# DeltaNet and a gated FFN on one core: K of two more chunks turned by VectorE, and the whole order planned anew

## The chip, the cores and the metric

The kernel runs on one core of a Trainium2 chip. The core's engines used here are TensorE (PE: matmuls, with its weight loads PEld), VectorE (DVE), ScalarE (ACT), GpSimd (POOL) and SyncE (SP, which here issues most DMAs). Each has an instruction queue of its own that it works through in order; semaphores make one wait for another. The time is the device time of one execution in microseconds. A lower time is better.

## The reference

```
def _attn_ref(q, k, v, beta):                 # (4, 8, 768, 48) each, beta (4, 8, 768)
    k_n = k / (np.linalg.norm(k, axis=-1, keepdims=True) + 1e-06)
    state = zeros((B, H, D, D))
    for t in range(S):
        kt, vt, bt = k_n[:, :, t], v[:, :, t], beta[:, :, t, None]
        y[:, :, t] = einsum('bhd,bhde->bhe', q[:, :, t], state)
        v_old = einsum('bhde,bhd->bhe', state, kt)
        state = state + bt[:, :, :, None] * einsum('bhd,bhe->bhde', kt, vt - v_old)
...
def _moe_ref(x, w_gate, w_val, w_out, rms_g): # x is y as (3072, 384)
    xn = x / sqrt(mean(x * x) + 1e-06) * rms_g
    g = xn @ w_gate                            # (384, 1536)
    return (g * sigmoid(g) * (xn @ w_val)) @ w_out
```

There are 32 heads of 48 numbers and 768 steps in time. All is fp32, except that the three weight matrices arrive as float64.

## The kernel before

**Tiling.** Time is cut into 12 chunks of 64 steps, numbered 0 to 11 here and in the code, so that the seventh and eighth chunk are 6 and 7. Within a chunk the recurrence is done as matrix products: the keys are normed (`norms`), K and Q are turned so that the head's numbers lie on the partitions (`kt`, `qt`), scores K·K and K·Q are formed on TensorE (`score_products`, L704), the triangular system of the chunk is solved on VectorE in 15 double steps (`invert`: multiply at L1070, reduce at L1076, after a scaling at L1023), the solution goes through DRAM into block form (`dx`, `dxt` to `mt`, `x2bd`, `m1bd`), and `recur` does the products with the state (L1199), the solve's application (L1281, evacuated at L1351), the output (L1317) and the state's update (L1404, added at L1522). The chunk's 256 output rows are then normed, turned and sent through the FFN. Chunks 0 and 1 use plain FFN matmuls (`ffn_plain`, L1558 and L1540). From chunk 2 on, `ffn` does the three by three block product with 15 products per half (L1651), whose results VectorE adds (L1661) and ACT copies (L1663), and `down` does a Strassen-like product with the output weights (L1708).

**How K is turned.** `kturn(c)` scales K on GpSimd (L969) and then takes one of two ways, by the constant `KSQ`. For `c < KSQ`, `turn` has TensorE transpose eight 128x128 blocks into two PSUM banks (L685), which ACT copies to `kt` (L697). For later chunks K is written to DRAM (`dsq`), read back in four DMAs with its 32x32 squares put at their turned places in the tile `q2`, and VectorE transposes every square in one instruction (`square_turn`, L715). Q of chunk 2 and later has always gone that way: 16 DMAs bring it from DRAM into the same tile `q2`, and the same L715 turns it into `qt`. So K's squares must wait until Q's have been turned, and the other way round.

**The first stretch.** The first chunks, the conversion of 18 pieces of float64 weights to fp32 by VectorE (L607, L610, L615, L639, with an ACT step at L619) and the FFN of chunks 0 and 1 share the time before the steady state. In the first 70 planned microseconds TensorE is fed idle matmuls on the identity in every planned gap (`filler`, L1826).

**What sets the order.** No order is written out by hand. Every operation is recorded in a `Plan` with its engine, a cost in microseconds, what it reads and writes, its PSUM banks and a priority or due time. `Plan.run` makes a list schedule (`forward`), goes back through it to set new priorities (`backward`), and repeats this `ROUNDS[0]` times with random shifts. Then each number in `MOVES` is the seed of one random change of the priorities (`shake`), after which the schedule is made again. The best schedule found by the planner's own costs is emitted, and each engine's queue holds its instructions in that order. So the costs in `P.add` move no work themselves, but they decide which instruction stands before which. A DMA has an issue cost (`dur`) on its queue and a cost on the shared DMA engines (`work`).

Of the kernel before, what the change touches and what calls it, by code (L numbers as in the profile page):

```python
# [22 lines left out]
STRETCH = {"PE": 1.5, "ACT": 1.5, "DVE": 1.4, "POOL": 1.2, "SP": 1.0}  # L23
ENGINES = ("PE", "ACT", "DVE", "POOL", "SP")
OVERLAP = {"PE": 0.0, "ACT": 0.1, "DVE": 0.08, "POOL": 0.06, "SP": 0.0}
ROUNDS, MOVES = (8, 3), (8000067, 8000597, 8000948, 8001017, 8002724, 8006360, 8008220, 8019300, 8029128, 8041120, 8046040, 8061420, 8103060, 8171660, 8171980, 8172520, 8176051, 8186548, 8187777, 8188940, 8197021, 8197169, 8200311, 8221546, 8225628, 8270861, 8283640, 8284428, 8285760, 8285870, 8288410, 8295221, 8301729, 8305291, 8310247, 8324080, 8458740, 8499977, 8522895, 8527737, 8540674, 8542770, 8573880, 8576584, 8577340, 8579620, 8580620, 8594840, 8603040, 8637560, 8655411, 8656870, 8664720, 8672920, 8873930, 8885129, 8893086, 8956398, 8960108, 9314698, 9382016, 9442358, 9601943)
BLOCK, ASKED, LACKED = 256, 140, 193
REACT, TURN, LAND = 2.4, 3.45, 2.6
STICK = 1.0
JKQ, JQM, JTM, JMK = 3, 99, 5, 99  # L30
EARLYN = (3, 4)
RELEASE = (4.7, 10.0, 13.0, 16.0, 16.0, 30.0, 33.0)
KSQ, XSQ = 8, 4
DRAIN, REFILL, GRACE = 0.1, 0.2, 0.0
SHAKE = 0.12
SPARE = 0.5
# [308 lines left out]
def kernel(  # L345
# [17 lines left out]
    nc = tc.nc  # L363
# [21 lines left out]
    half = sbt("half", [128, 16])  # L385
# [23 lines left out]
    q2t = q2.rearrange("p x e -> p (x e)").rearrange("p (u g th e) -> p u g th e", u=8, g=2, th=2)  # L409
    q2k = [("q2", i) for i in range(16)]  # L410
# [19 lines left out]
    AK = [("acc", 0), ("acc", 1)]  # L430
# [17 lines left out]
    ms = sbt("ms", [128, 2, 2], 2)  # L448
    rs = sbt("rs", [128, 2], 2)
# [29 lines left out]
    P = Plan()  # L479
    V = lambda n: 0.13 + 0.0011 * n  # L480
    VF = lambda n: 0.13 + 0.0006 * n
    A = lambda n: 0.2 + 0.0008 * n
    G = lambda n: 0.15 + 0.0022 * n

    def dma(dst, src, prio, r=(), w=(), work=0.3, dur=0.5, eng="SP", after=0.0):
        queue = nc.scalar if eng == "ACT" else nc.sync
        op = P.add(eng, dur, lambda: queue.dma_start(out=dst, in_=src), prio, r, w, lat=0.7)  # L487
        op.dma, op.work, op.ready, op.port = True, work, after, False
        return op

# [2 lines left out]
    def due(c, lead):  # L493

        return (64.0 - min(lead, 64.0)) if c == 0 else (90.0 if c == 1 else 152.9 + PERIOD * (c - 2)) - lead
# [156 lines left out]
    def load(c, what):  # L652
        t0 = c * C
        pk, pq, pv = ((-5, 1, 12), (5, 29, 36))[c] if c < 2 else (due(c, 150), due(c, 99), due(c, 70))
        if "q" in what and c > 1:
            for d, eh, g, th in itertools.product(range(2), repeat=4):
                e0, e1 = 32 * eh, min(D, 32 * eh + 32)
                src = q.rearrange("b (yh a) t e -> a t (b yh) e", a=4)[2 * d + g, t0 + 32 * th : t0 + 32 * th + 32, :, e0:e1]
                r0 = 64 * d + 32 * eh
                dma(q2t[r0 : r0 + 32, :, g, th, 0 : e1 - e0], src, pq, w=[q2k[8 * d + 4 * eh + 2 * g + th]], work=0.33 if eh else 0.43, after=due(c, 85))  # L660
        for key, t, src, pr in (("k2", k2[c % NK], k, pk), ("q2", q2, q, pq)):
            for g in range(2):
                if key[0] not in what or key == "q2" and c > 1:
                    continue
                dst = t[64 * g : 64 * g + 64, :, 0:D]
                s = src.rearrange("b (y g) t e -> g t (b y) e", g=2)[g, t0 : t0 + C]
                op = dma(dst, s, pr, w=[(key, c % NK, g)] if key == "k2" else q2k[8 * g : 8 * g + 8], dur=0.7, work=1.18, eng="ACT" if c == 0 and (g or key == "q2") else "SP", after=((0.0, 1.4, 0.0), (5.0, 40, 0.0))[c]["kqv".index(key[0])] if c < 2 else 44.5)
                op.lat += LATE if c == 1 or key == "q2" else 1.2 if c == 0 else 0.0
        if "v" in what and c < 2:
            for g in range(2):  # L670
                s = v.rearrange("b (y g) t e -> g t (b y) e", g=2)[g, t0 : t0 + C]
                dma(vt[64 * g : 64 * g + 64], s, pv, w=[("v", g)], dur=0.7, work=1.18, after=30 if c else 8).lat += LATE
        elif "v" in what:
            for bb in range(2):
                s = v[2 * bb : 2 * bb + 2, :, t0 : t0 + C, :].rearrange("p h t e -> t (p h) e")
                dma(vt[64 * bb : 64 * bb + 64], s, pv, w=[("v", bb)], dur=0.85, work=1.18, after=due(c, 75))
# [106 lines left out]
    def prep16(c):  # L783
        pr = 8.0 if c == 1 else 0.0
        pd = pr + (1 if c else 0)
        pi = (1.0, 45.0)[c]
        i2, ikq = c, c
# [10 lines left out]
        psf = Group()  # L798
# [57 lines left out]
        ab = [("ab", c, n) for n in range(4)]  # L856
        ak = [("acc", c)]
# [15 lines left out]
                nc.scalar.copy(flat(side)[:, L * c : L * c + 33 * 15 + 1 : 33], share())  # L873

        P.add("ACT", 0.6, start, pd, r=["half"], w=ak)
        P.add("ACT", 0.4, start2, pd + 0.5, r=[psf], w=ak, last=psf)
        x, xkeys = x16[c], [("xs", c)]
        diag = a16[c].rearrange("p j t -> p (j t)")[:, 1 : 1 + 34 * 7 + 1 : 34]
        pair = x.rearrange("p i t -> p (i t)")[:, 0:128].rearrange("p (j k) -> p j k", k=L // 2)
# [17 lines left out]
        for j in range(0, L - 2, 2):  # L897
            n, m = j + 2, L - 2 - j

            def step(j=j, n=n, m=m):  # L900
                old, new, lo = (3, 0, 1) if j % 4 else (0, 3, 0)
                cols = slice(L * c + j + 2, L * c + L)
                nc.vector.tensor_tensor(
                    out=acc[:, 1:3, 0:n, cols].rearrange("p a i t -> p i a t"),
                    in0=sides[old][:, 0:n, j : j + 2, None].to_broadcast([128, n, 2, m]),
                    in1=a16[c][:, None, j : j + 2, j + 2 : L].to_broadcast([128, n, 2, m]),
                    op=ALU.mult,
                )
                nc.vector.tensor_reduce(
                    out=acc[:, new, 0:n, cols],  # L910
                    in_=acc[:, lo : lo + 3, 0:n, cols].rearrange("p a i t -> p i t a"),
                    axis=AXL.X,
                    op=ALU.add,
                )

            P.add("DVE", 0.47 + 0.0052 * n * m, step, pi, r=ab, w=ak)

        xflat = x.rearrange("p i t -> p (i t)")

# [5 lines left out]
                else:  # L925
                    nc.vector.tensor_copy(out=dst, in_=src)

        P.add("ACT" if c else "DVE", 0.97 if c else 0.55, spread, pi, r=ak, w=xkeys)
        P.add("DVE", V(256), lambda: nc.vector.transpose(out=turned[1], in_=xflat), pi, r=xkeys, w=["turn1"])
        psb = Group()  # L930

# [12 lines left out]
        for h in range(2):  # L944
            dst = dg[c][:, 8 * h : 8 * h + 8].rearrange("p x (n m) -> p x n m", n=4)
            src = lambda h=h: psb.t[:, 128 * h : 128 * h + 128].rearrange("p (x m) -> p x m", x=8)[:, :, None].to_broadcast([128, 8, 4, L])
            w = [("dg", c, h)] + (kkall if c else [])
# [62 lines left out]
    def invert(c):  # L1010
        pd = due(c, 110) + 1
        pi = due(c, 80)
        i2, ikk = c % 2, c % 2
        dk = dkk[c % 2]
        dkeys = [("dkk", c % 2, g, i) for g in range(2) for i in range(2)]
        for par in range(2):
            dma(at_[64 * par : 64 * par + 64].rearrange("p j t -> p (j t)"),
                dk.rearrange("i g x j t -> (i g x) (j t)"), pd, r=dkeys, w=[("at", par)] + [(n_, p_, z) for n_ in ("ab",) for p_ in range(2) for z in range(4)] + [("xs", 0), ("xs", 1)], dur=0.56, work=0.95)
        bt = beta_b[:, c]
        bkeys = [("beta", i) for i in range(8)]  # L1020

# [14 lines left out]
                        bt[rows, par : W : 2],  # L1036
                    )

        P.add("ACT", 1.0, start, pd, r=["half"], w=AK)
        P.add("ACT", 0.9, start2, pd + 0.5, r=bkeys, w=AK)  # L1040


# [22 lines left out]
        for j in range(0, W - 2, 2):  # L1065
            n, m = j // 2 + 1, W - 2 - j

            def step(j=j, n=n, m=m):
                old, new, lo = (3, 0, 1) if j % 4 else (0, 3, 0)
                nc.vector.tensor_tensor(  # L1070
                    out=acc[:, 1:3, 0:n, j + 2 : W].rearrange("p a i t -> p i a t"),
                    in0=acc[:, old, 0:n, j : j + 2, None].to_broadcast([128, n, 2, m]),
                    in1=at_[:, None, j : j + 2, j + 2 : W].to_broadcast([128, n, 2, m]),
                    op=ALU.mult,
                )
                nc.vector.tensor_reduce(  # L1076
                    out=acc[:, new, 0:n, j + 2 : W],
                    in_=acc[:, lo : lo + 3, 0:n, j + 2 : W].rearrange("p a i t -> p i t a"),
                    axis=AXL.X,
                    op=ALU.add,  # L1080
                )

            P.add("DVE", 0.47 + 0.0052 * n * m, step, pi, r=[("at", 0), ("at", 1)], w=AK)

        def spread(dst, op, turn):
            for side in range(2):
# [90 lines left out]
    def recur(c):  # L1177
# [245 lines left out]
        for h in halves:  # L1423
            gy = groups(psy, h)

            if c == 0:
                p = h[0]
                for g in range(2):
                    P.add("ACT", A(192) + 0.15, lambda p=p, g=g: nc.scalar.activation(
                        out=xflat[:, 128 : 320], in_=psy[g, p].t[:, 192 * p : 192 * p + 192], func=ACTF.Square,  # L1430
                        scale=1.0 / math.sqrt(DM), accum_out=ms[i2][:, p, g : g + 1],
                    ), py, r=[psy[g, p]], w=[("x1", 1), ("ms", i2, p)], last=psy[g, p])
# [21 lines left out]
                    nc.gpsimd.tensor_scalar(out=ms[i2][:, cols, 0], in0=ms[i2][:, cols, 0], scalar1=ms[i2][:, h[0], 1:2], scalar2=1e-6, op0=ALU.add, op1=ALU.add)  # L1454
                nc.gpsimd.tensor_tensor(out=rs[i2][:, cols], in0=ms[i2][:, cols, 0], in1=mhalf[:, cols], op=ALU.pow)

            P.add("POOL", 1.1, root, py, r=["half"], w=[(k_, i2, p) for p in h for k_ in ("ms", "rs")])
            if c == 0:
                p = h[0]
                P.add("DVE", V(128), lambda p=p: nc.vector.tensor_scalar(  # L1460
# [401 lines left out]
```

## Time and profile before

| | |
|---|---|
| time, median of 3 runs | 673.76 us (672.74 to 675.8) |
| profiled execution, its own time | 673.21 us |
| its span, first to last instruction | 671.5 us |
| TensorE busy | 657.3 us, 98% of the span, granted clock 0.994 |
| VectorE busy | 577.0 us, 86% |
| ACT busy | 298.2 us, 44% |
| POOL busy | 88.5 us, 13% |
| K and Q transposes on TensorE, L685 | 64 and 16 matmuls |
| square transposes on VectorE, L715 | 10 for Q at 1.238 us, 4 for K at 1.241 us |

An engine's busy time is the time in which it has an instruction under way; for TensorE the ends are modelled, since its matmuls overlap. The profiled execution's time is 1.7 us longer than its span, for what lies before the first and after the last instruction. A wait is shown with the instruction that waited, what released it, its total, how often and the longest. The chain of waits follows the last instruction back to what released it, and so on; each piece has its start, its length and its line. In a table of windows each row has the stretch, its length, the busy time and instructions of PE, PEld, DVE, ACT and POOL, the granted TensorE clock, the DMA engines' share and GB/s.

### The profile page before, as it was taken

Reading aid. Unit: us, or ns where it says so; the run is one execution under the profiler, and the core shown is the slowest. Engines: PE = TensorE matmul, PEld = TensorE weight load, DVE = VectorE, ACT = ScalarE, POOL = GpSimd, SP = SyncE. Lnnn points to the kernel's source line nnn. Section 1 sums busy time; section 2 is a strip of 40 time slices with the busy share of each in tenths; the row PEclk is TensorE's granted clock in tenths of the full one; section 3 lists DMA queues with packets and bytes.
Section 4 is the critical chain, followed back from the end, with each engine's and each line's share of the span. In section 5 each row is a group of like instructions: output and inputs, shape, how many; then the busy total and the mean of one; then the engine's idle time right before and its main releaser. Section 6 shows DMA issues by size and latency. Waiting matters only on the chain.

```text
span 671.5 us, 23512 instructions
## 1 busy us (share of the span) xinstructions
PE 657.3 (98%) x10070; PEld 608.2 (91%) x10070; DVE 577.0 (86%) x1199; ACT 298.2 (44%) x685; POOL 88.5 (13%) x105
## 2 busy tenths in 40 slices
PE   9899989999999999999999999999999999999997
PEld 6788768787799999999999999999999999999997
DVE  6999889999999998997998898899998798457472
ACT  7554343454235455355345345345345354343241
POOL 4212211050300040040031030030040010000000
PEclk9999979999999999999999999999999999999999
DMA  9483666573325336345347456476346434102100
GB/s 233 125 221 108 135 166 167 91 146 75 48 63 79 63 84 107 57 99 91 54 123 109 76 132 96 82 168 97 48 117 92 84 79 70 26 2 48 24 1 24
DMA packets 261822, 62.31 MB, mean 93 GB/s; under 512 B 248627, under 2 KB 253782, under 8 KB 261718
## 3 DMA queue, kind: packets, MB, share of 16 engines
q1 hardware_dynamic: 258438, 60.02, 45.5%
q8 instruction: 79, 1.29, 0.8%
q10 hardware_dynamic: 3280, 0.79, 0.6%
q14 instruction: 25, 0.20, 0.1%
HBM read 44.25 MB, written 16.52 MB: 91 GB/s over the span
## 4 chain that ended last, share of the span: by engine, by line
PE 79%; DVE 12%; SPq 3%; DMA 2%; issue 2%; ACT 1%; POOL 1%; DVEq 0%; POOLq 0%
PE bank L1651 36%; PE bank L1708 19%; PE bank L1558 7%; PE bank L1540 4%; PE bank L704 3%; PE bank L1199 3%; SPq L487 3%; PE bank L1281 1%; PE bank L1317 1%; DVE tmp L1661 1%; DVE acc L1076 1%; PE bank L685 1%; PE bank L1404 1%; PE bank L1124 1%; DVE acc L1070 1%
## 5 line engine op out<-in xcount | busy, mean ns | idle before, releaser
L1651 PE MATMUL bank<-xf,w_in 128*128 128x128 f32 x1440 | 177.4, 276 | 0.0
L1651 PEld LDWEIGHTS bank<-xf,w_in 128*128 128x128 f32 x1440 | 168.7, 192 | 0.8
L1661 DVE TENSOR_TENSOR tmp<-tmp,bank 128x512 f32<-128x512 f32 x180 | 121.3, 683 | 34.6 <-PE bank L1651 30.2
L1651 PE MATMUL bank<-xf,more 128*128 128x128 f32 x960 | 123.8, 277 | 0.0
L1651 PEld LDWEIGHTS bank<-xf,more 128*128 128x128 f32 x960 | 115.1, 192 | 0.9
L1663 ACT COPY tmp<-bank 128x512 f32<-128x512 f32 x120 | 69.0, 584 | 63.0 <-PE bank L1651 49.4
L1667 ACT ACTIVATE tmp<-tmp 128x256 f32<-128x256 f32 x120 | 50.1, 417 | 93.7 <-DVE tmp L1661 93.2
L1076 DVE TENSOR_REDUCE acc<-acc 128x30 f32<-128x90 f32 (+4 forms) x150 | 70.9, 472 | 5.2
L731 POOL TENSOR_TENSOR knrm<-ksum,half 128x16 f32<-128x16 f32 x12 | 35.5, 2960 | 274.5 <-DVE ksum L730 274.5
L1708 PE MATMUL bank<-wo_sb,hf 128*128 128x192 f32 x360 | 63.8, 329 | 0.0
L1708 PEld LDWEIGHTS bank<-wo_sb,hf 128*128 128x128 f32 x360 | 58.1, 190 | 0.5
L1070 DVE TENSOR_TENSOR acc<-acc,at 128x60 f32<-128x60 f32 (+4 forms) x150 | 52.7, 351 | 2.4
L1668 DVE TENSOR_TENSOR hf<-tmp 128x256 f32<-128x256 f32 x120 | 49.0, 418 | 5.5 <-ACT tmp L1667 4.7
L1540 PE MATMUL bank<-wo_sb,hf 128*128 128x384 f32 x96 | 35.2, 506 | 0.0
L1558 PE MATMUL bank<-xf,w_in 128*128 128x256 f32 x144 | 34.6, 387 | 0.0
L1558 PE MATMUL bank<-xp,w_in 128*128 128x256 f32 x144 | 33.4, 383 | 0.0
L1558 PEld LDWEIGHTS bank<-xp,w_in 128*128 128x128 f32 x144 | 26.8, 190 | 4.6 <-DVE more L1616 0.2
L1558 PEld LDWEIGHTS bank<-xf,w_in 128*128 128x128 f32 x144 | 26.4, 190 | 4.4 <-issue 0.2
L1713 ACT COPY tmp<-bank 128x192 f32<-128x192 f32 x30 | 9.5, 316 | 41.7 <-PE bank L1708 41.2
L1540 PEld LDWEIGHTS bank<-wo_sb,hf 128*128 128x128 f32 x96 | 18.3, 196 | 9.9 <-issue 0.6
L1096 POOL COPY acc<-acc 128x128 f32<-128x128 f32 x40 | 18.8, 500 | 63.1 <-DVE acc L1076 62.8
L1510 DVE TENSOR_TENSOR xf<-xf 128x256 f32<-128x256 f32 (+1 forms) x70 | 24.7, 381 | 2.5 <-ACT xf L1475 1.9
(198 smaller groups left out, 985.8 us busy)
## 6 DMA issues: line engine op xcount, KB each, us to landing
at<-dkk SPq DMA_DIRECT2D x20, 256.0 KB, 3.7
more<-in_moe_w_gate_dram SPq DMA_DIRECT2D x6, 768.0 KB, 7.6
vt<-in_v_dram SPq DMA_DIRECT2D x24, 192.0 KB, 4.0
k<-in_k_dram SPq DMA_DIRECT2D x23, 192.0 KB, 4.2
out_dram<-tmp SPq DMA_DIRECT2D x46, 96.0 KB, 2.2
more<-in_moe_w_val_dram SPq DMA_DIRECT2D x5, 768.0 KB, 8.4
more<-in_moe_w_out_dram SPq DMA_DIRECT2D x5, 768.0 KB, 5.5
dyn<-yn SPq DMA_DIRECT2D x16, 192.0 KB, 2.0
```

The source lines that it names most:

```text
L731: P.add("POOL", 2.95, lambda: nc.gpsimd.tensor_tensor(out=knrm[i2], in0=ksum[i2], in1=half, op=ALU.pow), pn, r=[("ksum", i2), "half"], w=[ ...
L1070: nc.vector.tensor_tensor(out=acc[:, 1:3, 0:n, j + 2 : W].rearrange("p a i t -> p i a t"), in0=acc[:, old, 0:n, j : j + 2, None].to_broadc ...
L1076: nc.vector.tensor_reduce(out=acc[:, new, 0:n, j + 2 : W], in_=acc[:, lo : lo + 3, 0:n, j + 2 : W].rearrange("p a i t -> p i t a"), axis=A ...
L1510: P.add("DVE", V(128 * n), lambda dst=dst, a=a, b_=b_, op=op: nc.vector.tensor_tensor(out=dst, in0=a, in1=b_, op=op), pxv, r=[("xp", 0)], ...
L1540: nc.tensor.matmul(po[p].t[:, 0:DM], hf[:, spot(f), 128 * p : 128 * p + 128], wo_sb[:, spot(f)], start=(f == f0), stop=(f == f1 - 1), skip ...
L1558: nc.tensor.matmul(ps.t[:, TOK * side : TOK * side + TOK], w_in[:, side, h_, 3 * t + i_, n : n + 128], x_[:, 2 * t : 2 * t + 2].rearrange( ...
L1651: nc.tensor.matmul(g.t[:, 128 * z : 128 * z + 128], fac[:, side, 128 * f : 128 * f + 128], xf[:, xs], start=(begin and z == 0), stop=False ...
L1661: P.add("DVE", V(512), lambda t=t, g=g: nc.vector.tensor_tensor(out=t, in0=t, in1=g.t, op=ALU.add), -1, r=[g], w=[tk], last=g)
L1663: P.add("ACT", A(512), lambda t=t, g=g: nc.scalar.copy(t, g.t), -1, r=[g], w=[tk], last=g)
L1667: P.add("ACT", A(256), lambda t=t: nc.scalar.activation(out=t[:, 0:256], in_=t[:, 0:256], func=ACTF.Silu), -1, w=[tk])
L1668: P.add("DVE", V(256), lambda t=t, f0=f0, p=p: nc.vector.tensor_tensor(out=hf[:, spot(f0) : spot(f0) + 2, 128 * p : 128 * p + 128], in0=t[ ...
L1708: nc.tensor.matmul(g.t[:, 0:192], a_[:, f], b_[:, f], start=(begin and f == 0), stop=(f == 5), skip_group_check=True)
```

## The change

`KSQ` goes from 8 to 6, so K of chunks 6 and 7 takes the way through DRAM and VectorE that chunks 8 to 11 take already. The planner gets other costs: SP's DMA issues cost 0.08 more, Q's 16 small loads and the two loads of the scores get another share of the DMA engines, a solver step costs 0.10 less, and some ACT and POOL operations cost less. Seed and rounds of the planner change, and the list of moves is another and longer one (from 63 to 141 seeds). No operation is computed in another way, apart from K's turns; but since the order is planned anew, every engine's queue differs nearly from its start.

```diff
-ROUNDS, MOVES = (8, 3), (8000067, 8000597, 8000948, 8001017,
+ROUNDS, MOVES = (9, 18), (9000793, 9000810, 9000860, 9001460,
...
-KSQ, XSQ = 8, 4
+KSQ, XSQ = 6, 4
...
     def dma(dst, src, prio, r=(), w=(), work=0.3, dur=0.5, eng="SP", after=0.0):
         queue = nc.scalar if eng == "ACT" else nc.sync
-        op = P.add(eng, dur, lambda: queue.dma_start(out=dst, in_=src), prio, r, w, lat=0.7)
+        op = P.add(eng, dur + (0.08 if eng == "SP" else 0.0), lambda: queue.dma_start(out=dst, in_=src), prio, r, w, lat=0.7)
...
# load, Q from chunk 2 on
-                dma(q2t[...], src, pq, w=[...], work=0.33 if eh else 0.43, after=due(c, 85))
+                dma(q2t[...], src, pq, w=[...], work=0.2 if eh else 0.25, after=due(c, 85))
...
# prep16, chunks 0 and 1
-        P.add("ACT", 0.4, start2, pd + 0.5, r=[psf], w=ak, last=psf)
+        P.add("ACT", 0.3, start2, pd + 0.5, r=[psf], w=ak, last=psf)
-            P.add("DVE", 0.47 + 0.0052 * n * m, step, pi, r=ab, w=ak)
+            P.add("DVE", 0.37 + 0.0052 * n * m, step, pi, r=ab, w=ak)
-        P.add("ACT" if c else "DVE", 0.97 if c else 0.55, spread, pi, r=ak, w=xkeys)
+        P.add("ACT" if c else "DVE", 0.75 if c else 0.42, spread, pi, r=ak, w=xkeys)
...
# invert, chunks 2 and later
-                dk.rearrange("i g x j t -> (i g x) (j t)"), pd, r=dkeys, w=[...], dur=0.56, work=0.95)
+                dk.rearrange("i g x j t -> (i g x) (j t)"), pd, r=dkeys, w=[...], dur=0.56, work=1.3)
-        P.add("ACT", 1.0, start, pd, r=["half"], w=AK)
+        P.add("ACT", 0.5, start, pd, r=["half"], w=AK)
-            P.add("DVE", 0.47 + 0.0052 * n * m, step, pi, r=[("at", 0), ("at", 1)], w=AK)
+            P.add("DVE", 0.37 + 0.0052 * n * m, step, pi, r=[("at", 0), ("at", 1)], w=AK)
...
# recur
-                    P.add("ACT", A(192) + 0.15, lambda p=p, g=g: nc.scalar.activation(
+                    P.add("ACT", 0.33, lambda p=p, g=g: nc.scalar.activation(
...
-            P.add("POOL", 1.1, root, py, r=["half"], w=[(k_, i2, p) for p in h for k_ in ("ms", "rs")])
+            P.add("POOL", 1.1 if c else 0.7, root, py, r=["half"], w=[(k_, i2, p) for p in h for k_ in ("ms", "rs")])
```

More of the change, by code (lines that the diff above doesn't have):

```diff
@@ L25 @@
 OVERLAP = {"PE": 0.0, "ACT": 0.1, "DVE": 0.08, "POOL": 0.06, "SP": 0.0}
-ROUNDS, MOVES = (8, 3), (8000067, 8000597, 8000948, 8001017, 8002724, 8006360, 8008220, 8019300, 8029128, 8041120, 8046040, 8061420, 8103060, 8171660, 8171980, 8172520, 8176051, 8186548, 8187777, 8188940, 8197021, 8197169, 8200311, 8221546, 8225628, 8270861, 8283640, 8284428, 8285760, 8285870, 8288410, 8295221, 8301729, 8305291, 8310247, 8324080, 8458740, 8499977, 8522895, 8527737, 8540674, 8542770, 8573880, 8576584, 8577340, 8579620, 8580620, 8594840, 8603040, 8637560, 8655411, 8656870, 8664720, 8672920, 8873930, 8885129, 8893086, 8956398, 8960108, 9314698, 9382016, 9442358, 9601943)
+ROUNDS, MOVES = (9, 18), (9000793, 9000810, 9000860, 9001460, 9001960, 9002345, 9002460, 9003400, 9004200, 9005000, 9005360, 9005563, 9007566, 9007573, 9009163, 9009249, 9011520, 9012804, 9012960, 9013220, 9014060, 9014129, 9015760, 9018380, 9019512, 9020480, 9022334, 9023780, 9023880, 9026340, 9026605, 9026722, 9027018, 9027166, 9027548, 9028780, 9031580, 9033520, 9037400, 9040880, 9042900, 9042908, 9043710, 9048160, 9049080, 9051340, 9059160, 9060309, 9062164, 9062577, 9064697, 9064993, 9066100, 9066824, 9079169, 9094180, 9103942, 9106506, 9107934, 9108247, 9108464, 9108495, 9110305, 9153718, 9154640, 9154926, 9156227, 9156781, 9157531, 9157562, 9157620, 9158560, 9159400, 9162020, 9163540, 9163922, 9164039, 9165075, 9165340, 9169026, 9170179, 9175407, 9175424, 9179280, 9179781, 9180194, 9182999, 9183612, 9197113, 9200469, 9203880, 9203917, 9204454, 9205160, 9205840, 9249400, 9340401, 9340560, 9340697, 9342077, 9450708, 9450960, 9450980, 9451255, 9451269, 9452102, 9452250, 9452367, 9452656, 9452663, 9453554, 9454370, 9455055, 9455280, 9455351, 9455533, 9455781, 9457357, 9457380, 9457488, 9458734, 9458740, 9461883, 9464820, 9465693, 9466085, 9470659, 9530753, 9557126, 9557422, 9557570, 9557976, 9558272, 9558420, 9558864, 9558881, 9559294, 9561903, 9562113, 9562526, 9562691)
 BLOCK, ASKED, LACKED = 256, 140, 193
@@ L659, in load @@
                 r0 = 64 * d + 32 * eh
-                dma(q2t[r0 : r0 + 32, :, g, th, 0 : e1 - e0], src, pq, w=[q2k[8 * d + 4 * eh + 2 * g + th]], work=0.33 if eh else 0.43, after=due(c, 85))
+                dma(q2t[r0 : r0 + 32, :, g, th, 0 : e1 - e0], src, pq, w=[q2k[8 * d + 4 * eh + 2 * g + th]], work=0.2 if eh else 0.25, after=due(c, 85))
         for key, t, src, pr in (("k2", k2[c % NK], k, pk), ("q2", q2, q, pq)):
@@ L1017, in invert @@
             dma(at_[64 * par : 64 * par + 64].rearrange("p j t -> p (j t)"),
-                dk.rearrange("i g x j t -> (i g x) (j t)"), pd, r=dkeys, w=[("at", par)] + [(n_, p_, z) for n_ in ("ab",) for p_ in range(2) for z in range(4)] + [("xs", 0), ("xs", 1)], dur=0.56, work=0.95)
+                dk.rearrange("i g x j t -> (i g x) (j t)"), pd, r=dkeys, w=[("at", par)] + [(n_, p_, z) for n_ in ("ab",) for p_ in range(2) for z in range(4)] + [("xs", 0), ("xs", 1)], dur=0.56, work=1.3)
         bt = beta_b[:, c]
```

## The prediction

> **What bounds the kernel now.** I read the page first, then the windows, the engines' waits and the chain.
>
> ```profile
> PE 657.3 (98%) x10070; PEld 608.2 (91%) x10070; DVE 577.0 (86%) x1199; ACT 298.2 (44%) x685; POOL 88.5 (13%) x105
> 110.00:130.00 20.00, 20.00 (x126) 15.19 (x125) 19.21 (x40) 9.44 (x21) 0.00 (x0) 1.00 0.64 144
> 150.00:170.00 20.00, 20.00 (x308) 15.59 (x307) 19.79 (x34) 9.00 (x25) 0.00 (x0) 1.00 0.32 66
> 210.00:230.00 20.00, 20.00 (x246) 18.83 (x248) 19.69 (x41) 10.42 (x29) 0.00 (x0) 1.00 0.49 81
> ```
>
> TensorE is busy 98% of the span. The windows' columns are PE, PEld, DVE, ACT, POOL, clock: from 110 to 230 us VectorE is as full as TensorE. Over 109 to 225 us VectorE's waits come to 0.4 us, and TensorE's after 91 us to 0.4 us. Before 90 us it is different:
>
> ```profile
> PE bank L704 <- DVE qt L715: 3.3, 1, 3.3
> ...
> DVE at L1023 <- DMA q<-in_q_dram: 2.6, 1, 2.6
> ...
> 88.00:90.00 2.00, 0.00 (x0) 0.00 (x0) 1.88 (x5) 0.15 (x1) 0.69 (x1) 0.89 1.06 369
> 92.00:93.00 1.00, 1.00 (x21) 0.82 (x15) 0.93 (x3) 0.00 (x0) 0.00 (x0) 0.50 0.39 44
> 97.00:98.00 1.00, 1.00 (x7) 0.87 (x6) 0.93 (x3) 1.00 (x2) 0.00 (x0) 1.00 0.00 0
> ```
>
> At 87.25 us TensorE stops for the turned Q of chunk 2 (3.28 us), because VectorE had waited 2.65 us at 79.9 for the scores' transfer. After the stop the granted clock is 0.50 until about 96 us. The chain prices both, and the groups used below:
>
> ```profile
> 90.53 1.98 PE bank L704 x64
> 92.51 2.86 PE bank L1540 x4
> 95.37 1.44 PE bank L685 x8
> 96.80 2.59 PE bank L1558 x12
> 99.40 1.09 PE bank L704 x64
> 115.82 1.29 PE bank L1540 x4
> 145.22 0.87 PE bank L685 x8
> 630.68 22.33 PE bank L1651 x200
> 655.85 11.71 PE bank L1708 x72
> ```
>
> The first three groups cost 1.09, 1.29 and 0.87 us at full clock, so the half clock cost 0.89 + 1.57 + 0.57 = 3.03 us.
>
> **Two sums.** T is TensorE's work in its order at such prices (L1651 0.112 us each, L1708 0.163), warming matmuls of L1826 left out. V is VectorE's work in its order at the mean of each shape, less 0.07 us where instructions overlap; the short solver steps L1070 and L1076 get 0.03 more. Check: between the scalings L1023 at 115.86, 167.68 and 222.63 V gives 51.7 and 54.8 us; the trace has 51.8 and 55.0. T over the whole kernel is 624.0, and TensorE ends at 667.57, so 43.5 us of its time is no work: 26.4 by the scores of Q(2) (T 64.1), 3.0 of half clock, the rest mostly some 0.25 us at each change between whole and split rows. VectorE's idle time is 8.2 us by 80 us, 10.8 after that wait, and 13.6 by 222 us.
>
> **The change, part by part.**
>
> *K of chunks 6 and 7* (the seventh and eighth). Sixteen TensorE transposes go: 2 x 0.87 = 1.74 us of the bound engine. Four ACT copies (L697, 0.582 us) go from an engine at 44%: nothing. Two VectorE transposes of 1.24 us come, and ten DMAs on SP. One square turn needs from the end of Q's turn (403.48) to the start of K's (411.48) 8.0 us for its loads. SP is in order: the stores of the inverse (`dxt`, `dx`) and the gathers for L1473 (`yn`) stand behind the store (0.60 us) and the four loads (0.68 each), so they move by up to 3.3 us a chunk; chunks 8 to 11 carry the same and TensorE waits for nothing there, so 0, with 6.6 as the end covered by the last rival. POOL's scaling of K (L969) stands ahead of either way. The new order leaves 12.3 and 13.5 us of VectorE work between Q's turn and K's turn of chunks 6 and 7: no wait. It is 8.6 at chunk 11: bounds 0 and 0.6 us, I take 0. The bounds of this part are -1.74 (VectorE has room) and +0.74 (2 x 1.24 on the path); rows say room, since VectorE waits 2.7 us for others from 225 to 300 us.
>
> The Trainium skill, "VectorE: DVE Perf Modes", section "Rules for kernel authors", speaks against this part: it sends a 128x128 transpose to TensorE when PSUM will do, as VectorE only turns 32x32 blocks. Here the rows have 0.87 us of TensorE against 1.24 of VectorE; by the rule the total would be 2.5 us higher, by the rows it stands.
>
> *Order up to 100 us.* The new order puts the scores of Q(2) at T 78.4 in place of 64.1, behind the chunk's products with the state and 14 us of FFN matmuls. V at the end of that turn is 91.5 in place of 79.2. With 8.2 us idle VectorE is done at 99.7; TensorE arrives at 78.4 + 22.3 = 100.7. (22.3: the 23.1 it had before the stop, less 0.8, by which V less T is smaller at the last product of chunk 1, L1317: 14.1 for 14.9. Warming matmuls shrink from 42 to 34 units of 128 columns, some 0.22 us each, but VectorE sets that stretch.) Were the 2.65 us wait for the scores' transfer back, the stop would be 1.6 us. VectorE has 4.1 us more work before L1023, so I take no stop. Gone: 3.28 + 3.03 + 0.8 = 7.1 us. Late next is VectorE itself.
>
> The Trainium skill, "TensorE: Matmul & The Clock Gate", Part 1, has the clock halve after an idle window of about 3.4 us and return after as long a busy one. The trace agrees that a stop this long halves it, but half clock lasted 5.7 us of work: by the page it would cost 1.7 us, by the rows 3.03, and the rows decide.
>
> *What VectorE takes back.* At T 214.7 before, V is 233.1; with 13.6 idle that is 246.7, and TensorE is there at 247.7: hardly ahead. So TensorE can be earlier only as far as VectorE is. The new order at T 212.0 has V 232.7. VectorE's idle time lies between 8.2 (nothing of the 5.4 us lost after 80 us comes back) and 10.9 (half of it does): TensorE passes at 240.9 to 243.6, before at 212 + 32.9 = 244.9. The gain left there is 1.3 to 4.0; I take 2.7, so 4.4 of the 7.1 are lost.
>
> A reason lies in the costs: a solver step L1070 + L1076 of 8 x 16 takes 1.09 us (94.73 to 95.82), the planner's old cost less its overlap of 0.08 is 1.06, the new 0.96. Fifteen steps a chunk are thus put some 2 us too short.
>
> *After 225 us.* In three stretches the new order has more V than T between a TensorE result and the next matmul needing VectorE: T 233.8 to 259.6 (V 27.3, T with changes 26.5), 339.7 to 361.0 (23.2, 21.9), 494.8 to 524.6 (31.2, 30.5): 2.8 us. Before, none exceeds. It is lost only if VectorE enters without a lead: 0 to 2.8, I take half, 1.4. Changes of rows after T 65 go from 57 to 56: nothing.
>
> *Transfers.* The edited costs (0.08 us per SP issue, `work` of loads) issue nothing; the order they make is counted above. Loads and stores of chunks 2 to 5 keep their number.
>
> **Sum.** On the profiled execution (673.21: span 671.5 and 1.7 around): -1.74 - 2.7 + 1.4 = -3.0, so 670.2. That execution is 0.55 below the median of 673.76, which would give 670.8; I put the forecast at 670.3, nearer the execution that the rows come from.
>
> **Rivals.**
> - *The early gain stays.* VectorE's idle time really falls to 8.2 and spare work is put off past 230 us: -7.1 - 1.74 + 1.4 = -7.4, about 665.8. For it: 5.4 us of VectorE's idle time came after 80 us. Against: the row of 246.7 and 247.7.
> - *All is eaten.* The three stretches lose 2.8, the early gain keeps 1.3: -0.2, about 673.0.
> - *Slower: K's turned copy comes late.* The round trip of chunk 6 or 7 meets loads (k<-in_k_dram lands in 4.2 us, the square's load took 5.1) and misses its place. Once it is more than 3.3 us late TensorE stops, as at 87.25, and pays 3.3 + 3.0. Both chunks: 670.3 + 2 x 6.3 = 682.9, one 676.6. Against: the slack of 12.3 and 13.5 for 8.0.
>
> **How the numbers follow.** What this measurement can tell from no change is about 0.5%, 3.4 us: faster ends at 670.4, slower starts at 677.1. My forecast (0.43, own range 668.3 to 672.3) sits on that line, so I split it evenly. Gain kept 0.26; all eaten 0.17; late K 0.14, of which 0.01 stays within the bound. Faster 0.215 + 0.26, so 0.48; same 0.39; slower 0.13. Range 664.8 to 675: it holds the first three cases but for their tails and a single short stop.
>
> **What would show it.** L685 has 48 matmuls on K, L715 six on `kt`. TensorE's wait on L715 near 90 us is gone and the clock row stays at 1.0. TensorE gets waits on VectorE (L1661, L1351, L1522) between 110 and 260 us, 3 to 5 us together, where it now has none; VectorE stays full there. I am wrong if the scores of Q(2) stop again, if L704 waits for L715 on `kt`, or if TensorE has no wait at all after 110 us (then 666).

## The result, and the profile after

The changed kernel takes 675.27 us (median of 20 runs, 673.05 to 679.29); the kernel before, over as many, 673.25. The ratio is 1.0031, 95% interval 1.0017 to 1.0045: about 2.1 us slower, where 670.3 was forecast (range 664.8 to 675.0). The profiled execution is a long one, 677.48 us with a span of 675.8, 2.2 above the median.

The page's busy line and the windows of the changed kernel; the columns are those of the prediction's windows.

```profile
PE 655.9 (97%) x10054; PEld 606.7 (90%) x10054; DVE 577.9 (86%) x1201; ACT 294.8 (44%) x681; POOL 90.1 (13%) x105
...
18.00:20.00 2.00, 0.56 (x4) 0.34 (x2) 1.83 (x8) 1.52 (x2) 0.00 (x0) 1.00 0.00 0
22.00:24.00 2.00, 2.00 (x42) 1.62 (x35) 2.00 (x4) 0.37 (x1) 0.00 (x0) 0.50 0.05 12
40.00:42.00 2.00, 2.00 (x10) 1.82 (x10) 1.04 (x3) 0.00 (x0) 0.00 (x0) 0.52 1.03 262
92.00:93.00 1.00, 1.00 (x27) 0.87 (x19) 0.93 (x3) 0.67 (x2) 0.00 (x0) 1.00 1.28 234
110.00:130.00 20.00, 20.00 (x115) 15.83 (x113) 18.25 (x35) 7.18 (x16) 0.00 (x0) 1.00 0.87 198
150.00:170.00 20.00, 19.22 (x356) 15.71 (x349) 19.32 (x38) 9.22 (x24) 4.59 (x6) 1.00 0.42 71
```

The half clock at 92 us is gone, as forecast. Two others have come that nobody counted, at 22 and 40 us, each behind some 2 us in which TensorE stood still. And TensorE is no longer full from 150 us on. Its waits by who ended them (total, times, longest), and the matmuls of K's turn:

```profile
PE bank L936 <- DVE w_in L929: 2.7, 2, 2.1
PE bank L1651 <- DVE tmp L1661: 2.4, 5, 0.6
PE bank L1826 <- issue: 2.0, 1, 2.0
...
PE bank L1317 <- DVE u L1351: 1.0, 1, 1.0
...
PE bank L1651 <- DVE state L1522: 0.7, 1, 0.7
PE bank L704 <- DVE kt L715: 0.5, 1, 0.5
...
L685 PE MATMUL bank<-ident,k 128*128 128x128 f32 x48 | 6.6, 277 | 0.9 <-DVE hf L1566 0.8 <-DMA k<-in_k_dram 0.2
```

The change does what it says: 48 transposes of K are left on TensorE. The first 45 us differ most. Kernel before, then changed:

```profile
0.00:45.00 45.00, 40.22 (x832) 32.49 (x832) 37.34 (x104) 28.01 (x55) 12.92 (x23) 1.00 0.77 189
45.00:80.00 35.00, 33.31 (x732) 27.74 (x732) 34.17 (x58) 16.58 (x33) 4.86 (x3) 1.00 0.54 131
```

```profile
0.00:45.00 45.00, 37.46 (x821) 31.92 (x822) 34.19 (x97) 25.31 (x51) 12.60 (x23) 0.92 0.73 177
45.00:80.00 35.00, 33.89 (x671) 28.40 (x671) 34.28 (x60) 18.18 (x34) 5.55 (x2) 1.00 0.62 157
```

By 80 us VectorE has idled 8.5 us before (7.66 + 0.83) and 11.5 after (10.81 + 0.72), and TensorE is 2.8 us less busy in the first 45. The 3.0 us more of VectorE's idle time all lie in the first 45.

The turned Q of chunk 2 and its scores in the changed kernel: VectorE's wait ahead of the scaling L1023 (89.24 us), VectorE's turn, and TensorE behind it.

```profile
DVE at L1023 <- issue: 1.3, 1, 1.3
...
103.70 1.24 DVE qt L715
...
105.00 1.15 PE L1199 MATMUL bank<-state,qt 48*64 48x48 f32 x64 [1.20 <-DVE qt L715]
105.97 1.13 PE L704 MATMUL bank<-qt,kt 64*64 64x64 f32 x64
```

**Set against the plan.** Every operation has a planned start. The kernel's own plan ends at 666.3 us before and at 661.8 after, so by its costs the change gains 4.5 us. The table has how much later than planned VectorE's operations start, counted from the first instruction that works, mean of each stretch, in the profiled executions. The last two columns belong to experiments below.

| planned time, us | before | changed | step_cost | after_costs_ksq8 |
|---|---|---|---|---|
| 20 to 40 | -0.4 | 1.3 | -0.3 | 1.9 |
| 40 to 60 | -0.7 | 3.9 | 0.5 | 6.3 |
| 100 to 120 | 3.7 | 4.4 | 2.7 | 7.1 |
| 210 to 240 | 2.6 | 6.8 | 2.1 | 6.0 |
| 420 to 450 | 3.6 | 11.3 | 1.6 | 7.3 |
| 600 to 630 | 3.3 | 11.5 | 1.5 | 9.3 |

The kernel before runs along with its plan but for one step of some 4 us between 75 and 110, around the stop at 87.25 us and its half clock. The changed one falls behind by 3.9 in the first 45 us: it is 1.4 late in what is planned for 30 to 35 us, and 2.4 more come by 40 to 45, behind the stop at 36.6 us and its half clock. From 120 to 450 it loses 6 to 7 more in this long execution, and 4.2 in early_fill below, which has all but the same order and was profiled at its median.

### The profile page after: what moved, and what is told of

Read it like the earlier page. It is cut to its first block, busy times and chain, and to the rows that moved or that the text cites. A ratio compares the mean times of both kernels' runs of the same rounds, so it can differ in the third digit from the quotient of the medians.

```text
span 675.8 us, 23483 instructions
## 1 busy us (share of the span) xinstructions
PE 655.9 (97%) x10054; PEld 606.7 (90%) x10054; DVE 577.9 (86%) x1201; ACT 294.8 (44%) x681; POOL 90.1 (13%) x105
## 4 chain that ended last, share of the span: by engine, by line
PE 62%; DVE 23%; DMA 5%; issue 4%; SPq 3%; ACT 1%; POOL 0%; DVEq 0%; ACTq 0%; POOLq 0%
PE bank L1651 32%; PE bank L1708 18%; DVE acc L1076 4%; SPq L487 3%; DVE acc L1070 3%; PE bank L704 3%; PE bank L1199 2%; DVE tmp L1661 2%; PE bank L1558 1%; DMA out_dram<-tmp 1%; PE bank L1317 1%; DMA at<-dkk 1%; DMA q<-in_q_dram 1%; DVE qt L715 1%; DVE more L1616 1%
## 5 line engine op out<-in xcount | busy, mean ns | idle before, releaser
L1667 ACT ACTIVATE tmp<-tmp 128x256 f32<-128x256 f32 x120 | 49.7, 417 | 99.7 <-DVE tmp L1661 99.5
L731 POOL TENSOR_TENSOR knrm<-ksum,half 128x16 f32<-128x16 f32 x12 | 37.7, 3141 | 314.5 <-DVE ksum L730 314.5
L1076 DVE TENSOR_REDUCE acc<-acc 128x30 f32<-128x90 f32 (+4 forms) x150 | 70.9, 473 | 5.2
L1070 DVE TENSOR_TENSOR acc<-acc,at 128x60 f32<-128x60 f32 (+4 forms) x150 | 52.6, 350 | 2.4
L1540 PE MATMUL bank<-wo_sb,hf 128*128 128x384 f32 x96 | 34.8, 493 | 0.6 <-DVE hf L1566 0.5
L1540 PEld LDWEIGHTS bank<-wo_sb,hf 128*128 128x128 f32 x96 | 17.4, 190 | 9.5 <-DVE hf L1566 0.6
```

The lines of the kernel that those rows point to most:

```text
L731: P.add("POOL", 2.95, lambda: nc.gpsimd.tensor_tensor(out=knrm[i2], in0=ksum[i2], in1=half, op=ALU.pow), pn, r=[("ksum", i2), "half"], w=[ ...
L1070: nc.vector.tensor_tensor(out=acc[:, 1:3, 0:n, j + 2 : W].rearrange("p a i t -> p i a t"), in0=acc[:, old, 0:n, j : j + 2, None].to_broadc ...
L1076: nc.vector.tensor_reduce(out=acc[:, new, 0:n, j + 2 : W], in_=acc[:, lo : lo + 3, 0:n, j + 2 : W].rearrange("p a i t -> p i t a"), axis=A ...
L1540: nc.tensor.matmul(po[p].t[:, 0:DM], hf[:, spot(f), 128 * p : 128 * p + 128], wo_sb[:, spot(f)], start=(f == f0), stop=(f == f1 - 1), skip ...
L1667: P.add("ACT", A(256), lambda t=t: nc.scalar.activation(out=t[:, 0:256], in_=t[:, 0:256], func=ACTF.Silu), -1, w=[tk])
```

## The experiments

Ratios are to the kernel before run on the same chip, with their 95% interval; the changed kernel's is 1.0031 (1.0017 to 1.0045). 0.001 is 0.67 us.

### The gap at 18.56 us

```diff
-                    filler(fillers(pe, s))
+                    filler(fillers(pe, s) + ([4, 4] if op.n == 91 else []))
```

> The changed kernel with its order kept, and with two more warming matmuls of 512 columns (1.8 us) ahead of the first L936, in the gap of 2.12 us at 18.56 us. Theory: the clock stays at 1.0 from 21 to 25 us, L848 takes 1.08 in place of 1.84 us and L956 1.12 in place of 1.95, so TensorE is 1.2 to 1.6 us earlier at 25 us. If that passes to the end: 673.7 to 674.1. Rival: the next gap (the first L1485 waits, at 36.6 us) takes it all, 675.3, and the half clock of 38 to 42 us is still there. A third: the two matmuls shift the instruction fetch and the gap at 36.6 us is another size.

Measured: 674.45 us, 1.0032 (1.0020 to 1.0045), no change. The half clock at 22 us went, and VectorE ran 0.7 us earlier from 40 us on. The stop at 36.6 us stayed, but moved. TensorE's timeline (start, length, line; in brackets the idle time before), changed kernel first, then this one:

```profile
35.19 0.68 PE L1317 MATMUL bank<-u,pt 64*64 64x48 f32 x32
35.80 0.81 PE L1826 MATMUL bank<-ident 128*128 128x256 f32 x3
38.65 0.37 PE L1826 MATMUL bank<-ident 128*128 128x128 f32 x1 [2.03 <-issue]
```

```profile
34.47 0.68 PE L1317 MATMUL bank<-u,pt 64*64 64x48 f32 x31
37.21 0.20 PE L1317 MATMUL bank<-u,pt 64*64 64x48 f32 x1 [2.06 <-issue]
```

Two matmuls more ahead of it (four records, since each fp32 matmul has two) put the stop four records earlier in the stream: before the last L1317, no longer before the fourth L1826. So it hangs on a count of instructions, not on any result. In the changed kernel a packet of the instruction queue, 16 KB, was under way from 35.9 to 37.3 us, and in this one from 34.8 to 35.8: both times TensorE goes on 1.3 to 1.4 us after its end. That TensorE waited for this packet is argued from that, not shown.

### The stop at 87.25 us, alone

In the kernel before, the scores of Q(2) go behind five later groups of TensorE.

```diff
+        at = [op.n for op, _ in best[1]]
+        late, after = at.index(420), at.index(457)
+        best[1].insert(after, (best[1].pop(late)[0], best[1][after - 1][1] + 1.31))
         for op, s in best[1]:
```

> The kernel before with its order kept but for one move: the scores of Q(2), L704 at 90.5 us, stand behind the two L1540/L1558 groups, the L685 of K(3) and the L1558 group that follow them, so that TensorE has 5 us of work before it needs the turned Q. The stop of 3.28 us and the half clock (3.03 us) should go. By the prediction's step VectorE takes back 4.4 of 7.1, so about 1.9 less than 673.25: 671.3. Rival, the gain stays: 667. Other rival, VectorE is so full from 90 to 225 us that all of it goes into waits there: 673.

Measured: 672.55 us beside 672.06, ratio 1.0000 (0.9985 to 1.0015). Nothing is gained, as the second rival had it. The wait on the turned Q is gone, but another result of the same late VectorE took its place (line numbers are three higher here: L1540 and L1566):

```profile
PE bank L1543 <- DVE hf L1569: 2.7, 1, 2.7
```

The other half of what I had priced, the half clock, is not fixed by the order. Each execution has a mean granted clock. Of the kernel before, among the 29 executions run beside this one, 4 had 1.0 and took 670.8 us on average, 15 had 0.997 and took 672.0, 6 had 0.994 and took 673.3: none, one or two pieces of 3.4 us at half clock (the other four lie between, at 0.995 and 0.996). The profile that the prediction was made from was one of the last kind. With the scores moved the same three kinds took 670.1 (one execution), 671.8 and 673.2. Nor does half clock make the changed kernel's loss: its five executions with 1.0 took 674.9 on average, beside 675.27 for the median of all.

### VectorE's lateness in the first 50 us

```diff
-            op.fn()
+            if op.n not in (155, 156, 161, 162, 167, 168):
+                op.fn()
```

> The changed kernel with its order kept, but with L607 and L610 left out for the three weight pieces whose conversion is planned between 42 and 52 us (six instructions of 0.55 us, 3.3 us of VectorE; the weights of these pieces come out wrong). It gives VectorE back what it is late by at 45 us against its own plan (3.8 us). Theory A, the loss of the first 50 us passes to the end because VectorE is full from 50 to 225 us: 2.5 to 3.3 us less than the changed kernel's 675.3, so 672.0 to 672.8. Rival B, what is lost after 110 us comes whatever lead VectorE brings: 0 to 1 us less, 674.3 to 675.3.

Measured: 672.7 us, ratio 1.0002 (0.9985 to 1.0018): 2.0 us less than the changed kernel. That is short of A's 2.5 to 3.3 and beyond B's 1. In the trace VectorE was 3.9 us earlier between 50 and 80 us than in the changed kernel. The lead passes on, though not whole. It is not all due to what was left out: VectorE was 2.3 us earlier already ahead of the first piece left out, since TensorE's stop at 36.3 us was 1.58 us here and no half clock followed it.

### VectorE from 110 us on

```diff
             def step(j=j, n=n, m=m):
+                if c > 2 and j in (12, 14):
+                    return
```

> The changed kernel with its order kept, and two of the 15 solver steps (the ones of 7x18 and 8x16, L1070 and L1076, about 2.2 us) left out in chunks 3 to 11; the solution is then wrong. Theory: from 110 to 520 us TensorE loses 8.4 us more than in the kernel before, to VectorE results that come late because a solver step is costed 0.12 us too short, 1.8 us a chunk. Then this takes 5 to 8 us off 675.3: 667 to 670. Rival, the loss is in transfers, fetches and changes of rows: at most 1.5 us less, 674.

> The kernel before with its order kept, and the same two solver steps (7x18 and 8x16) left out in chunks 3 to 11; the solution is then wrong. It is the control of the run that takes them out of the changed kernel, which gained 0.86% (1.0031 to 0.9945 of before, some 5.8 us). Theory, late VectorE results are what the new order has and the old one has not: 0.5 to 2 us less than before. Rival, VectorE limits both orders alike: 5 to 6 us less.

Measured: the changed kernel falls to 668.9 us, ratio 0.9945 (0.9930 to 0.9959), 5.8 us less. The kernel before stays where it was, 1.0005 (0.9985 to 1.0024), where 0.5 to 2 us less was expected. The same 2.2 us of VectorE a chunk is worth 5.8 us to one order and nothing to the other. TensorE's column shows where, changed kernel first, then the one with two steps less:

```profile
150.00:200.00 50.00, 48.13 (x613) 40.01 (x606) 48.42 (x96) 19.59 (x46) 9.35 (x8) 1.00 0.38 67
...
246.00:300.00 54.00, 52.81 (x844) 50.89 (x843) 48.36 (x103) 26.48 (x64) 9.18 (x11) 1.00 0.56 107
...
360.00:430.00 70.00, 68.63 (x1090) 65.79 (x1089) 61.48 (x128) 32.33 (x77) 7.06 (x8) 1.00 0.60 103
```

```profile
150.00:200.00 50.00, 49.48 (x600) 41.41 (x592) 48.13 (x98) 20.42 (x49) 8.04 (x7) 1.00 0.38 67
...
246.00:300.00 54.00, 54.00 (x861) 52.60 (x861) 47.43 (x101) 26.68 (x64) 7.67 (x10) 1.00 0.60 113
...
360.00:430.00 70.00, 70.00 (x1165) 67.32 (x1164) 60.64 (x128) 31.04 (x78) 7.17 (x8) 1.00 0.54 99
```

With the steps out, VectorE stays 2 to 3 us behind the plan from 120 us to the end. The slip is gone. This shows that late VectorE results make it, and not yet why they are late.

### K's turns by themselves

```diff
-            op.fn()
+            if op.n not in (*range(1332, 1338), *range(1567, 1573)):   # changed kernel
+            if op.n not in (*range(1332, 1336), *range(1565, 1569)):   # kernel before
+                op.fn()
```

> The kernel before with its order kept, with the turns of K of chunks 6 and 7 left out: 16 transposes L685 and four ACT copies L697; these chunks then work with the turned K of chunks 4 and 5. It measures the first term of the prediction by itself. Prediction's theory, TensorE is the bound there: 1.74 us less. Rival, VectorE sets the pace from 240 to 300 us: 0 to 0.5 us less.

> The changed kernel with its order kept, with the other way of K of chunks 6 and 7 left out: two stores to DRAM, eight loads and two VectorE transposes L715 (2.48 us); these chunks then work with the turned K of chunks 4 and 5. Prediction's theory, all of it lies beside other work: 0 to 0.5 us less than the changed kernel (the one TensorE wait on the turned K of chunk 6 was 0.5 us). Rival, VectorE is the bound there: 2.5 us less, and more if the round trip delays the chunk too.

Measured: without its 16 transposes the kernel before has 0.9976 (0.9958 to 0.9995), 1.6 us less, as predicted. Without its way through DRAM the changed one has 1.0018 (1.0001 to 1.0034), 0.9 us less than 1.0031; the two intervals overlap, so a cost of 0 to 2 us. The turns thus save 1.6 and cost about 0.9, which is not clear of noise.

### The planner's costs

In the two traces a solver step (L1070 and L1076, start to next start, mean 0.81 us) takes some 0.06 us more than the new cost less its overlap, and some 0.04 less than the old. It takes 0.13 more than the new cost where the next VectorE operation is the next step, and 0.02 more where another stands between. Over 164 steps the change makes VectorE 16 us shorter in the plan; some 10 of that are not there on the chip. These four have a new search each, with the same seeds for the start.

```diff
 # step_cost: both places
-            P.add("DVE", 0.37 + 0.0052 * n * m, step, ...)
+            P.add("DVE", 0.43 + 0.0052 * n * m, step, ...)
 # after_costs_ksq8
-KSQ, XSQ = 6, 4
+KSQ, XSQ = 8, 4
 # measured_costs, and measured_costs_ksq8 with KSQ 8
+FIX = {("ACT", 622): 0.085, ..., ("ACT", 1030): 0.65, ..., ("DVE", 1071): 0.055, ...}
...
+        for op in self.ops:
+            op.dur += FIX.get((op.eng, op.fn.__code__.co_firstlineno), 0.0)
```

> The changed kernel with one cost alone set right, the solver step (0.43 in place of 0.37, both places), and a new search of the same kind (21 moves kept); planner's end 667.8. Theory: the step is the largest of the too small costs (9 of 23.8 us), so the slip falls from 13.5 to between 8 and 11: 676 to 679. Rival, it is nearly all of it: 674.5.

> The changed kernel's own costs, with KSQ 8 and a new search of the same kind (18 moves kept); planner's end 667.0. It has the costs of the change without its K turns. Theory, the costs make the slip: 11 to 13.5 us more than the plan, 678 to 680.5. Rival, K's way through DRAM makes it: 7 us more, 674.

> The changed kernel with the planner's costs of 28 kinds of VectorE and ACT operations set to what they took in the two traces (solver step 0.055 to 0.06 more, the scaling start L1028 on ACT 0.65 more, and so on; 23.8 us of VectorE over the kernel), and the order searched anew from the same seed with 600,000 random moves (84 kept). The planner's own end is 665.7, where it was 661.8 for the changed kernel and 666.3 for the one before; the chip took 13.5 us and 7.0 us more than that. Theory, costs too small make TensorE wait for late VectorE results: the chip takes 5 to 7 us more than the plan, 670.7 to 672.7, and VectorE's start times run along with the plan from 120 to 430 us within 2 us (in the changed kernel they slipped by 5 to 7). Rival, the turned K or a searched order as such brings the slip: 679.

> The same costs and the same search with KSQ 8, so K of chunks 6 and 7 is turned by TensorE as before; planner's end 668.1. Theory: 5 to 7 us more on the chip, 673 to 675, so 1 to 2.4 us more than with KSQ 6. Rival, the way of K costs what it saves: no difference to KSQ 6, or less.

Measured, beside 672.47 us of the kernel before:

| | planner's end | chip, us | more than planned | ratio (95%) |
|---|---|---|---|---|
| step_cost | 667.8 | 671.24 | 3.4 | 0.9983 (0.9969 to 0.9997) |
| after_costs_ksq8 | 667.0 | 676.62 | 9.6 | 1.0078 (1.0054 to 1.0102) |
| measured_costs | 665.7 | 670.66 | 5.0 | 0.9983 (0.9966 to 1.0000) |
| measured_costs_ksq8 | 668.1 | 669.96 | 1.9 | 0.9967 (0.9950 to 0.9984) |

One cost set right makes a plan that ends 6.0 us later on paper and 3.2 us earlier on the chip than the changed kernel (1.0031 to 0.9983); my theory had expected less of it, 676 to 679. The change's costs without its K turns keep the loss and more (676.6 lies between theory and rival), and the early lateness with it (6.3 us by 45 us, in the table above). So K's way is not what makes the loss. KSQ 8 with measured costs is no slower than KSQ 6, against my expectation of 1 to 2.4 us; the intervals overlap, so the K turns are worth nothing that shows here. measured_costs_ksq8 is the fastest of all, 0.33% or 2.2 us below the kernel before. TensorE's longest waits in step_cost, where none on VectorE is over 1.2 us:

```profile
PE bank L704 <- issue: 2.1, 1, 2.1
PE bank L685 <- DMA q<-in_q_dram: 1.5, 1, 1.5
...
PE bank L936 <- DVE w_in L929: 1.2, 1, 1.2
```

### The first chunks' steps, and the later ones'

```diff
 # step_cost_first: L916, chunks 0 and 1; step_cost_later: L1083, chunks 2 to 11
-            P.add("DVE", 0.37 + 0.0052 * n * m, step, ...)
+            P.add("DVE", 0.43 + 0.0052 * n * m, step, ...)
```

> The changed kernel with the solver step's cost set right (0.43) in chunks 0 and 1 alone, and a new search of the same kind (49 moves kept); planner's end 664.3. Theory, the step cost of the first two chunks makes the loss of the first 50 us and that of the later chunks the drift from 120 to 430 us: VectorE starts at most 1 us behind the plan at 45 us (3.7 in the changed kernel), and slips by 4 to 7 us more from 120 to 430; 9 to 11 us more than the plan at the end, 673 to 675. Rival, the later chunks' cost alone matters: early lateness of 3 us or more is still there.

> The other half: the step's cost set right in chunks 2 to 11 alone, chunks 0 and 1 left at 0.37; new search (45 moves kept); planner's end 668.0. Theory: 3 us or more behind the plan at 45 us, then within 1.5 us of that to the end; 6 to 9 us more than the plan, 674 to 677. Rival, the early lateness does not depend on the step's cost: 671, as with both set right (3.4 us more than the plan).

Measured: 673.07 us, ratio 1.0005 (0.9985 to 1.0025), and 674.19 us, 1.0028 (1.0011 to 1.0045). VectorE against the plan, us:

| planned time, us | step_cost_first | step_cost_later |
|---|---|---|
| 20 to 40 | -0.3 | 1.4 |
| 40 to 60 | 2.1 | 3.7 |
| 120 to 150 | 3.8 | 3.8 |
| 420 to 450 | 4.8 | 3.8 |
| 510 to 540 | 7.5 | 3.1 |

With the later chunks' cost right the drift is gone and the early lateness stays, as the theory had it. The other half is clean only at the start. In what is planned for 30 to 35 us VectorE is 1.3 to 1.4 us late in the changed kernel, step_cost_later and after_costs_ksq8, which all have 0.37 in chunks 0 and 1, and 0.4 to 1.3 early in the four orders with that cost set right; TensorE's wait ahead of L936 is 1.9 to 2.2 us in those and 1.1 to 1.2 in these. So the first chunks' cost makes some 2 us of lateness by 35 us. What comes behind is another thing: 2.1 us at 40 to 60 us was to be 1 at most, and this execution has an "issue" stop of 2.7 us ahead of L848 at 34.4 us; in step_cost the stop of 2.1 us comes only at 53 us. As for the drift, VectorE's lateness grows between 120 to 150 and 420 to 450 us by 0.7, 1.0 and 4.2 to 6.5 us in the three orders with 0.37 in the later chunks, and stays as it is or falls by up to 2.7 in the four with that cost right. So this cost makes the drift, but its size hangs on the order: 4 to 7 us was expected in step_cost_first, and 1.0 came, or 3.7 by 540.

## Why the prediction was wrong

- **K of chunks 6 and 7** (-1.74, bounds -1.74 and +0.74): right in its saving (1.6 measured), too hopeful in pricing ten DMAs and two transposes at nothing (some 0.9; where I took no wait, VectorE waited 1.0 us for the squares of chunk 6, and TensorE 0.5 for their turn; for chunk 7 there was none). The net of about -0.7 lies within the bounds and is not resolved.
- **The stop and its half clock gone** (7.1 us): gone in the trace, but never worth that. Moved alone in the old order they bring nothing. The 3.28 us was VectorE's lateness, and the next VectorE result asks for it again. The 3.03 us of half clock was one execution's: others of the same kernel have half of it or none, and all of it is worth 2.5 us at the end.
- **"With 8.2 us idle VectorE is done at 99.7"**: this is the step that failed, and it decides the result. VectorE was done with the turn of Q(2) at 104.9 (it starts at 103.70), 5.2 later; TensorE waited 1.2 for it, and came to the scores of Q(2) at 105.97 where I had 100.7. I had carried VectorE's idle time over from the old order as if it belonged to the kernel; it belongs to the order. Some 3.0 us of the 5.2 were lost in the first 45 us, which I had not costed at all. There the new plan has seven steps of chunk 0 too short by 0.7 us together (VectorE goes from 0.1 ahead to 0.6 behind its plan in what is planned between 15.1 and 18.9 us). TensorE then stands 2.12 us ahead of L936 (1.19 in the kernel before), runs at half clock, and meets a stop for instructions at 36.6.

  Another 2.1 us were lost between 83 and 90 us, where I took no wait: 0.5 and 0.3 us on TensorE's results, and 1.3 ahead of L1023. The last is where I had counted the wait for the scores' transfer as gone. The profile names no releaser for it, but the second half of that transfer was issued only at 85.34 us, behind six loads of Q, and with the median of 3.7 us from issue to landing it lands at 89.0 by estimate; L1023 starts at 89.24.

  Adding to the forecast the 5.3 us by which TensorE came late gives 675.6; 675.27 was measured. So near is partly luck: the profiled execution took 677.48, and with the two terms below its sum is 670.2 + 5.3 - 0.6 + 2.8 = 677.7. How much of such a delay reaches the end in other executions is not shown: early_dve_less gave VectorE 3.3 us back and brought 2.0.
- **What VectorE takes back**: right in size. From T 78 to 212 I had TensorE's time over T grow by 7.9 us; it grew by 7.3. The reason given, solver steps costed too short, was the right one, though I put it at some 2 us a chunk and the traces give 1.0: my 0.13 us a step holds only where the next operation is the next step. I had seen the cause and applied it to one stretch of three.
- **After 225 us** (+1.4, bounds 0 and 2.8): TensorE's time over T grew by 14.8 us from T 213 to the end in the profiled execution, where my terms come to 12.0, and by 12.4 in early_fill, which has all but the same order and ran at its median. The term was right but for what that one execution had besides.
- **Waits on VectorE of 3 to 5 us after 110**: seen, 5.0 us of TensorE not busy.
- **The signs that I would be wrong**: two of the three came. L704 waited for L715 on `kt` (0.5 us), and the turned Q of chunk 2 stopped TensorE again (1.2 us, at the L1199 just ahead of the scores).
- **The rivals**: the late K was a wait of 0.5 us, and no loss. The rival that was missing is that the new plan is worse because it believes costs the chip does not keep. I had named those costs, and priced the order as if the planner had merely found a better one.

What stays open: why one execution has a piece of half clock and the next has none, and what sets where a searched order meets its instruction stop, behind which 2.4 of the 3.8 us of early lateness came. The fill alone moved the median by nothing. Each set of costs also has one searched order here; how far two searches with the same costs would differ was not measured. That the four orders with the step's cost right at the start run 0.9967 to 1.0005, and the three with 0.37 there 1.0028 to 1.0078, speaks against luck of the search, and does not exclude it.

## What to carry to other kernels

A planned order is as good as its costs: before pricing what a new order wins, set each planned start against the start in the trace, and look for the first place where the two part. Where two engines are both nearly full, a duration put some 7% too short (0.06 us on a step of 0.81) can cost more than the stall that the search removes: setting it right was worth 3.2 us here, and the stop at 87.25 us nothing. A duration a little too long seems to leave slack: the old order, whose step is put some 0.04 us too long, kept to its plan but for that one stop. This was not tested by itself. A stall and a half clock in one profiled execution should be held against the clock of the other executions before they are counted as a gain.

## What the runs showed of the hardware

- TensorE's half clock comes in pieces of 3.41 us (from 21.4 and from 38.5 us in the changed kernel), behind stops of 2.12 and 2.03 us. In early_dve_less a stop of 1.58 us at the same place brought none, but length does not decide alone: the stop of 2.71 us in scores_later brought none either. The Trainium skill, "TensorE: Matmul & The Clock Gate", Part 1, has an idle window of about 3.4 us halve the clock and calls the window free-running. The length agrees, and so do the places in this trace: the two pieces start 17.07 us apart, five times 3.41. That the idle time must fill the window does not agree, since 2.1 us were enough here. In scores_later a boundary of such a row of windows falls inside the stop, with 1.0 us of it before and 1.7 behind; that it brought no half clock for this reason is not shown.
- What looks like a stop for instructions is part of the order. Nine of the fifteen profiles have one of 2.0 us or more on TensorE, put down to "issue" (L1826, L1317, L704 or L848 waits, by the order), the kernel before has none over 0.4 us, and early_fill moved it by as many records as it added.
